# A recurrence beside a mixture of experts on one core: token scaling, loads of B and K, and VectorE's order around Qc are moved

## The chip, the cores and the metric

The kernel runs on one core of one Trainium2 chip. The metric is the device time of one execution in microseconds (us). All inputs start in HBM and the result ends there.

A core has five engines that matter here, each with its own queue of instructions that it works through in order: TensorE (PE; its weight loads are shown as PEld), VectorE (DVE), ScalarE (ACT), GpSimd (POOL) and SyncE (SP), which here only issues DMAs. They wait for each other by semaphores.

## The reference

A delta-rule recurrence (RWKV-7) over 768 tokens runs for 4 batches and 8 heads of dimension 40. Its output, regrouped to 3072 rows of 320, goes through four small two-layer networks whose results are weighted and added.

```python
for t in range(S):                                   # S = 768; B, H, D = 4, 8, 40
    y[:, :, t] = np.einsum('bhd,bhde->bhe', rt, state)
    Sa = np.einsum('bhde,bhe->bhd', state, at)
    state = state * wt[:, :, None, :] - np.einsum('bhd,bhe->bhde', Sa, bt) + np.einsum('bhd,bhe->bhde', vt, kt)
x = y.transpose(0, 2, 1, 3).reshape(B * S, H * D)
p = domain_probs / (domain_probs.sum(-1, keepdims=True) + 1e-09)
for e in range(E):                                   # E = 4, w1[e] 320x1024, w2[e] 1024x320
    out += p[:, e:e + 1] * (np.maximum(x @ w1[e], 0.0) @ w2[e])
```

## The kernel before

**Units.** The recurrence is cut into 12 chunks of 64 tokens. A unit is one chunk of two batches, so there are 24 units (0 to 23), two for each chunk. Inside a unit the recurrence is turned into matrix products. Per unit there are three generators whose pieces are interleaved by hand: `within` (decays, scores, everything that needs no state), `merge` (the inverse of a triangular matrix) and `step` (what needs the state of the unit before).

**Decays.** The raw w of a unit is turned to channels by VectorE (`G`, L520, from the tile `rawW`), multiplied up along the tokens by a scan (L567), and inverted (`1/gp`, L582, 128x512, the reciprocal). From unit 8 on (`BY_CHANNEL`) the raw b and k are turned the same way (`Br`, `Kr`, L638, from `rawB`, `rawK` into the tiles NT and KT) and multiplied by the reciprocal: `N` (L640) and `K` (L644). a is turned and multiplied by the decays (`AT`, L624, and `AG`, L626). Each of rawW, rawB, rawK, rawA is a single tile that is loaded by four DMAs (`load_raw`, L285).

From unit 8 on, b and k are also loaded by tokens (`n_tok`, `k_tok`, L278). They need the same factor: TensorE transposes the reciprocal (pg), ScalarE copies it out (`decay`, L650), and GpSimd multiplies both by it (L727 to L730). That pair of products stands in `substitute`, behind the copies `below` and ahead of the copy of `unit_cols`.

**The triangular inverse.** TensorE makes the scores pfe from AT and NT, ScalarE copies them to F (L669). Two copies on VectorE and two on ScalarE take the diagonal blocks of F (`blocks`, L721). VectorE spreads them (`M`, L733, a transpose to 128x1024) and combines pairs of rows (`Z1`, `Z2`, L745, L749). Then GpSimd substitutes: 48 products and sums on Z (L763, L780). VectorE transposes the result twice (`Qc`, `QTc`, L791, L792) and GpSimd copies it to QT (L798). TensorE uses QTc in pY, Qc in pQ and QT in psat.

**The mixture.** The products of the four networks run on TensorE in pieces between the steps of the recurrence, in "gaps": `gap(n)` of the loop turn u runs one or two pieces. They are made with seven products for two 2x2 block matrices, for which VectorE makes five sums of the hidden values (`a`, L1102) per half expert and adds the results to the output (`osb`, L991). Each piece of w1 is 640 KB (one DMA of 512 KB, two of 64 KB) and is loaded into one of two tiles, w1a and w1b, by DMAs on SP that wait until TensorE has read the piece before.

**What sets the order.** On TensorE the order is that of the program (L110 keeps it). On VectorE a scheduler orders the instructions by its own estimates, but within pairs of the lists at L1433 to L1442: (one, then) means that `then` stands behind `one`. GpSimd's instructions in question are kept in program order. Loads that are put into the list `later` are issued on SP by `begin_later`: a few behind every piece of the mixture (L1184), and the rest where the loop says so. In loop turn u, unit u goes through `step`, unit u+1 through `merge`, unit u+2 through the later pieces of `within` and through `substitute`, and unit u+3 begins. Raw B and K of unit u+3 and W of unit u+4 are put into `later` at the end of turn u, behind `gap(3)`, so they are issued in `gap(0)` of the turn after.

Of the kernel before, what the change touches and what calls it, by code (L numbers as in the profile page):

```python
# [9 lines left out]
ALU = mybir.AluOpType  # L10
# [23 lines left out]
def kernel(  # L34
# [38 lines left out]
    nc = tc.nc  # L73

    B, H, S, D = r.shape
# [5 lines left out]
    NJ = H // 2  # L81
    NF = F // P
    NU = NC * B // 2
# [6 lines left out]
    def noted(ins, name, n=None, i=None):  # L90
        if n is None:
            n = sum(k.startswith(name) for k in made)
        key = f"{name}{n}" if i is None else f"{name}{n}.{i}"
        made[key] = ins
        if key in names:
            stated_order.append(ins)
        return ins
# [24 lines left out]
    def of_mixture(name):  # L122
# [6 lines left out]
        out=ident[:], in_=ident[:], pattern=[[1, P]], compare_op=ALU.is_equal, fill=0.0,  # L129
# [5 lines left out]
    for t, n, op in ((upf, L, ALU.is_gt), (diagf, Q, ALU.is_equal)):  # L135
        nc.vector.memset(t, 1.0)
        for q in range(P // n):
            o = slice(q * n, (q + 1) * n)
            nc.gpsimd.affine_select(
                out=t[o], in_=t[o], pattern=[[1, n]], compare_op=op, fill=0.0, base=0, channel_multiplier=-1,  # L140
# [87 lines left out]
    def pad_raw():  # L228
        for x in "BK":
            nc.gpsimd.memset(room[x][:, :, PAD:2 * D], 0.0)  # L230
# [25 lines left out]
    def begin(u):  # L256
        q = Unit()
        q.u, q.c, q.bp = u, u // (B // 2), u % (B // 2)
        q.b = [2 * q.bp, 2 * q.bp + 1]
        q.start, q.end = q.c == 0, q.c == NC - 1  # L260
        q.apart = u >= EARLY + 2
        q.n = {}
        units.append(q)
        return q
# [57 lines left out]
    def turn_raw(out, t):  # L322

        return nc.vector.transpose(
            out=out.rearrange("p n (x two) -> p n two x", two=2),
            in_=t.rearrange("p n (two e) -> p n two e", two=2)[:, :, :, 0:Q],
        )
# [173 lines left out]
    def within(q):  # L501
# [3 lines left out]
        def pin(ins, also=False):  # L505
            if q.u <= PADDED or also:
                keep(ins)
# [9 lines left out]
            q.G = Gv = flat[:, 0:2 * NJ * L].rearrange("p (c t) -> p c t", t=L)  # L517
            ahead = flat[:, 1:2 * NJ * L + 1].rearrange("p (j i t) -> p i j t", i=2, t=L)
        for i in range(2):
            pin(noted(turn_raw(ahead[:, i], n["rawW"][:, NJ * i:NJ * i + NJ, :]), "G", q.u, i), q.u > EARLY + 2)  # L520
        if by_channel:
            q.gl = G[:, :, L:L + 1]
        else:
# [109 lines left out]
        if by_channel:  # L633
            NT = sb.tile([P, 2 * NJ, L], FP32, name="NT", tag="turned", bufs=3)
            KT = sb.tile([P, 2 * NJ, L], FP32, name="KT", tag="turned", bufs=3)
            for t, x in ((NT, "B"), (KT, "K")):
                for i in range(2):
                    noted(turn_raw(t[:, i::2], n["raw" + x][:, NJ * i:NJ * i + NJ]), x + "r", q.u, i)  # L638
                if x == "B":
                    nc.vector.scalar_tensor_tensor(  # L640
                        out=t[:], in0=t[:], scalar=-1.0, in1=gp[:], op0=ALU.mult, op1=ALU.mult,
                    )
                else:
                    noted(nc.vector.tensor_tensor(out=t[:], in0=t[:], in1=gp[:], op=ALU.mult), "K", q.u)  # L644
        yield
# [70 lines left out]
    def substitute(q, eng, between=None, during=None, first=None):  # L716

        blocks = sb.tile([P, H, Q], FP32, name="blocks")
        for i in range(P // Q):
            move = nc.scalar.copy if i >= 2 else nc.vector.tensor_copy  # L720
            ins = move(out=blocks[quarter(i)], in_=q.F[quarter(i), :, quarter(i % 2)])  # L721
            keep(noted(ins, "blocks", q.u, i))
        run(first)
        q.below = belows()
        for i in (1, 3):
            tc.keep_in_program_order(nc.gpsimd.tensor_copy(out=q.below[quarter(i)], in_=q.F[quarter(i), :, 0:Q]))  # L726
        if q.u >= BY_CHANNEL:  # L727
            for x in (q.N, q.K):
                ins = nc.gpsimd.tensor_tensor(out=x[:, :, 0:D], in0=x[:, :, 0:D], in1=q.decay[:], op=ALU.mult)
                tc.keep_in_program_order(ins)  # L730
        M = sb.tile([P, Q, Q], FP32, name="M")
        cols = blocks[:].rearrange("p h c -> p c h")[:, :, None, :].to_broadcast([P, Q, 4, H])
        ins = nc.vector.transpose(out=M[:], in_=cols)  # L733
        keep(noted(ins, "M", q.u))


        pairs = M[:].rearrange("p (c two) r -> p c two r", two=2)
        on_diag = M[:].rearrange("p c r -> p (c r)")[:, Q + 1::2 * (Q + 1)]
        keep(noted(nc.vector.memset(on_diag, 0.0), "M0", q.u))

        Z = sb.tile([P, 4, Q // 4, Q], FP32, name="Z")
        q.Z = Z[:, 0]
        by_second = Z[:, 1:3].rearrange("p x k r -> p (x k) r")
        below = M[:].rearrange("p c r -> p (c r)")[:, 1::2 * (Q + 1)]
        ins = nc.vector.tensor_tensor(  # L745
            out=by_second, in0=pairs[:, :, 1, :], in1=below[:, :, None].to_broadcast([P, Q // 2, Q]), op=ALU.mult,
        )
        keep(noted(ins, "Z1", q.u))
        ins = nc.vector.tensor_tensor(out=pairs[:, :, 0, :], in0=pairs[:, :, 0, :], in1=by_second, op=ALU.add)  # L749
        keep(noted(ins, "Z2", q.u))  # L750
        run(between)
        at_once = eng is nc.vector
        for x in (0, 3) if at_once else (0,):
            if q.u < 2:
                noted(nc.scalar.copy(out=Z[:, x], in_=unit_cols[:]), "Zu", q.u, x)
            else:
                tc.keep_in_program_order(eng.tensor_copy(out=Z[:, x], in_=unit_cols[:]))
        for j in range(0, Q, 2):
            if during:
                during(j)  # L760
            n, m = j // 4 + 1, Q - 1 - j
            here = 3 * (j // 2 % 2) if at_once else 0
            ins = eng.tensor_tensor(  # L763
                out=Z[:, 1:3, 0:n, j + 1:Q], in0=M[:, j:j + 2, None, j + 1:Q].to_broadcast([P, 2, n, m]),
                in1=Z[:, here, 0:n, j:j + 2].rearrange("p k x -> p x k")[:, :, :, None].to_broadcast([P, 2, n, m]),
                op=ALU.mult,
            )
            noted(ins, "Zm", q.u, j)
            if j == 0:
                tc.keep_in_program_order(ins)  # L770
            z = Z[:, :, 0:n, j + 1:Q]
            if at_once:
                terms = z[:, 0:3] if here == 0 else z[:, 1:4]
                ins = eng.tensor_reduce(
                    out=z[:, 3 - here], in_=terms.rearrange("p x k r -> p k r x"), op=ALU.add, axis=AX.X,
                )
                noted(ins, "Zr", q.u, j)
            else:
                for x in range(1, 3):
                    eng.tensor_tensor(out=z[:, 0], in0=z[:, 0], in1=z[:, x], op=ALU.add)  # L780
        if at_once:

            odd, even = (Z[:, x].rearrange("p k (r four) -> p k r four", four=4)[:, :, :, 1:3] for x in (3, 0))
            eng.tensor_copy(out=even, in_=odd)

    def merge(q):

# [383 lines left out]
    def begin_later(n):  # L1171
        for move in later[:n]:
            tc.keep_in_program_order(move(nc.sync))
        del later[:n]
# [16 lines left out]
    def run(gen, n=99):  # L1191
        if gen is None:
            return
        for _ in range(n):
            if next(gen, gen) is gen:
                break
# [112 lines left out]
    for u in range(1, NU):  # L1309
# [9 lines left out]
        def gap(n, pieces=None):  # L1319
            here[0] = at = 4 * u + n  # L1320
            run(sum_ops, sums_at.get(at, 0))
            mix((1 if at in sparse else 2) if pieces is None else pieces)
# [46 lines left out]
        if u + 3 < NU:  # L1369
# [5 lines left out]
            if u > 1:  # L1375
                later.extend(load_raw(units[u + 3], "VR"))
        run(w, 2)

        soon = u in (2, 3, 4)
        if soon:  # L1380
# [28 lines left out]
        if early:  # L1409
            ws.append(within(units[u + 3]))  # L1410
            run(ws[u + 3], 1)
            if u > 1:
                run(m, 1)
                run(s_next, 1)
            run(m)
            if u == 3:
                begin_later(len(later))
            gap(3, 1)
            run(s_next, 1)
        else:  # L1420
            begin_later(len(later))
            gap(3)
        if BY_CHANNEL <= u + 3 < NU:
            if u + 3 == BY_CHANNEL:
                pad_raw()
            if u >= EARLY + 2 and u + 4 < NU:
                later.extend(load_raw(begin(u + 4), "W"))
            later.extend(load_raw(units[u + 3], "BK"))
        s = s_next
    mix(len(todo))  # L1430
    for piece in last:
# [2 lines left out]
    turned_ahead = [("Qc6", "RT7"), ("RT7", "QTc6")]  # L1434
    turned_ahead += [("QTc6", x) for x in ("VC7.0", "VC7.1", "sum_w15", "sum_w16")]
    waits_of_scalar = [(f"SXc0.{n}", "RTc1.0") for n in range(4)]
    ahead_of_merge = [(f"QTc{u - 1}", f"{x}r{u}.{i}") for u in range(BY_CHANNEL, NU) for x in "BK" for i in range(2)]
    ahead_of_merge += [(f"QTc{u - 1}", f"RH{u - 1}.{r}") for u in range(BY_CHANNEL, NU) for r in range(2)]
    ahead_of_merge += [(f"QTc{u - 1}", f"VC{u}.{r}") for u in range(BY_CHANNEL, NU) for r in range(2)]
    ahead_of_merge += [(f"1/gp{u + 2}", f"sum_a{10 * u - 45 + n}") for u in range(BY_CHANNEL, NU - 2) for n in range(5)]  # L1440
# [34 lines left out]
```

## Time and profile before

| | us |
|---|---|
| median of 3 runs | 1094.14 (1093.46 to 1099.57) |
| the profiled execution | 1094.94 |
| its span, from the first to the last instruction | 1092.8 |
| TensorE busy in the span | 1057.6 (97%) |
| VectorE busy | 812.2 (74%) |
| GpSimd busy | 543.6 (50%) |
| ScalarE busy | 343.3 (31%) |
| mean granted TensorE clock | 0.995 |

The profile is that of one execution. Times in it are us from the start of the span. A line of the timeline gives start, length, engine, line of the kernel, operation, what it writes and reads, shape, and how many instructions of the kind are merged; in brackets stands how long the engine was idle before, and what ended that. The list of waits gives the total of such idle times, how often, and the longest one.

TensorE is busy nearly throughout, so the time is made of its work plus the idle between. The other engines matter where they set that idle, or the order of the work.

### The profile page before, as it was taken

The page shows a single profiled execution, that of the slowest core. Times are in us where ns is not written, and L with a number is a line of the kernel's source. Part 1 is how long each engine was busy: PE and PEld are TensorE (multiplying, and loading weights), DVE is VectorE, ACT ScalarE, POOL GpSimd, SP SyncE. Part 2 cuts the span into 40 slices and gives each one's busy share as a digit, 9 for nine tenths or more (in the row PEclk, how much of TensorE's full clock was granted, in tenths as well). Part 3 has the DMA queues.
Part 4 walks back from the last instruction along what each step waited for, and adds up shares of the span by engine and source line. Part 5 has one row for each costly group of instructions (what it writes and reads, how often), then busy time and mean ns, then how long its engine had stood idle before and what let it go on. Part 6 is the DMA issues. An engine that isn't in the chain of part 4 may idle for free.

```text
span 1092.8 us, 38476 instructions
## 1 busy us (share of the span) xinstructions
PE 1057.6 (97%) x16022; PEld 947.0 (87%) x16022; DVE 812.2 (74%) x1565; ACT 343.3 (31%) x942; POOL 543.6 (50%) x1322
## 2 busy tenths in 40 slices
PE   7999999999999999999999999999999999999998
PEld 7778878989889889999989898898888888988888
DVE  7787779996877978878869788687797877543343
ACT  3433444332323333333323233233232332321110
POOL 6117778756356365465474473744735647430000
PEclk9999999999999999999999999999999999999999
DMA  6876543435443443543553543354444353121220
GB/s 117 213 191 130 136 106 105 106 81 107 118 91 97 106 108 90 112 107 87 119 110 66 131 111 74 84 128 84 101 116 94 87 112 91 38 82 57 67 91 13
DMA packets 275349, 111.04 MB, mean 102 GB/s; under 512 B 229816, under 2 KB 254952, under 8 KB 275176
## 3 DMA queue, kind: packets, MB, share of 16 engines
q1 hardware_dynamic: 271192, 107.75, 42.5%
q8 instruction: 126, 2.06, 0.8%
q10 hardware_dynamic: 3984, 0.84, 0.4%
q14 instruction: 47, 0.39, 0.1%
HBM read 100.65 MB, written 3.93 MB: 96 GB/s over the span
## 4 chain that ended last, share of the span: by engine, by line
PE 49%; POOL 27%; DVE 14%; issue 6%; SPq 2%; DMA 1%; ACT 1%; DVEq 0%; POOLq 0%; ACTq 0%
PE ph L110 21%; PE p L110 17%; POOL Z L780 17%; POOL Z L763 10%; DVE a L1102 3%; DVE M L733 3%; PE prn L110 2%; PE po L110 2%; DVE blocks L721 1%; DVE osb L991 1%; PE pdy L110 1%; DVE M L749 1%; DVE Z L745 1%; PE pY L110 1%; DVE Qc L791 1%
## 5 line engine op out<-in xcount | busy, mean ns | idle before, releaser
L780 POOL TENSOR_TENSOR Z<-Z 128x31 f32<-128x31 f32 (+7 forms) x704 | 257.9, 366 | 55.1
L110 PE MATMUL ph<-xT,w1b 128*128 128x256 f32 (+3 forms) x1536 | 225.1, 377 | 0.5 <-issue 0.5
L110 PE MATMUL ph<-xT,w1a 128*128 128x256 f32 (+3 forms) x1536 | 222.7, 375 | 0.0
L1102 DVE TENSOR_TENSOR a<-hs 128x512 f32<-128x512 f32 x220 | 159.6, 749 | 78.2 <-ACT hs L976 78.2
L976 ACT ACTIVATE hs<-ph 128x512 f32<-128x512 f32 (+1 forms) x208 | 116.5, 564 | 311.2 <-PE ph L110 309.2
L763 POOL TENSOR_TENSOR Z<-M,Z 128x62 f32<-128x62 f32 (+7 forms) x352 | 148.6, 422 | 100.1 <-DVE M L749 74.3
L110 PEld LDWEIGHTS ph<-xT,w1b 128*128 128x128 f32 (+1 forms) x1536 | 170.3, 163 | 28.8 <-issue 7.0
L110 PEld LDWEIGHTS ph<-xT,w1a 128*128 128x128 f32 (+1 forms) x1536 | 169.0, 162 | 29.0 <-issue 7.3
L110 PE MATMUL p<-sums,a 128*128 128x160 f32 x1056 | 164.9, 299 | 0.0
L991 DVE SCALAR_TENSOR_TENSOR osb<-p,gate,osb 128x320 f32<-128x320 f32 (+1 forms) x243 | 107.2, 479 | 64.3 <-PE p L110 61.0
L110 PEld LDWEIGHTS p<-sums,a 128*128 128x128 f32 x1056 | 152.8, 190 | 2.2
L726 POOL COPY below<-F 32x256 f32<-32x256 f32 x48 | 30.5, 636 | 202.5 <-ACT F L669 167.9
L110 PEld LDWEIGHTS p<-w,hs 128*128 128x128 f32 x704 | 98.6, 190 | 8.5 <-issue 7.3
L110 PE MATMUL p<-w,hs 128*128 128x160 f32 x704 | 104.9, 302 | 0.0
L110 PE MATMUL p<-w,a 128*128 128x160 f32 x704 | 102.8, 299 | 0.0
L110 PEld LDWEIGHTS p<-w,a 128*128 128x128 f32 x704 | 98.0, 190 | 0.0
L798 POOL COPY QT<-QTc 32x256 f32<-32x256 f32 x96 | 44.0, 458 | 60.6 <-DVE QTc L792 54.3
L896 ACT COPY RS<-pxr 64x256 f32<-64x256 f32 x88 | 32.3, 367 | 112.2 <-DVE SX L499 77.5
L791 DVE STREAM_TRANSPOSE Qc<-Z 128x256 f32<-128x256 f32 x24 | 14.9, 621 | 54.4 <-POOL Z L780 54.3
L582 DVE RECIPROCAL gp<-G 128x512 f32<-128x512 f32 x16 | 53.6, 3352 | 0.5
L707 ACT COPY EV<-pev 64x160 f32<-64x160 f32 x96 | 23.1, 286 | 83.0 <-PE pev L110 82.6
L733 DVE STREAM_TRANSPOSE M<-blocks 128x1024 f32<-128x1024 f32 x24 | 47.4, 1976 | 2.3 <-ACT blocks L721 0.6
(167 smaller groups left out, 1440.2 us busy)
## 6 DMA issues: line engine op xcount, KB each, us to landing
w1a<-in_moe_w_dram SPq DMA_DIRECT2D x37, 512.0 KB
w1b<-in_moe_w_dram SPq DMA_DIRECT2D x37, 512.0 KB
w<-in_moe_w_dram SPq DMA_DIRECT2D x4, 1280.0 KB
w1a<-in_moe_w_dram SPq DMA_DIRECT2D x74, 64.0 KB
w1b<-in_moe_w_dram SPq DMA_DIRECT2D x74, 64.0 KB
out_dram<-osb SPq DMA_DIRECT2D x45, 80.0 KB
rawW<-in_w_dram SPq DMA_DIRECT2D x48, 72.0 KB
natV<-in_v_dram SPq DMA_DIRECT2D x42, 80.0 KB
```

Of the source, the lines that this page charges most:

```text
L110: return stated(nc.tensor.matmul(**k))
L582: pin(noted(nc.vector.reciprocal(out=gp[:], in_=G[:, :, 1:L + 1]), "1/gp", q.u))
L726: tc.keep_in_program_order(nc.gpsimd.tensor_copy(out=q.below[quarter(i)], in_=q.F[quarter(i), :, 0:Q]))
L733: ins = nc.vector.transpose(out=M[:], in_=cols)
L763: ins = eng.tensor_tensor(out=Z[:, 1:3, 0:n, j + 1:Q], in0=M[:, j:j + 2, None, j + 1:Q].to_broadcast([P, 2, n, m]), in1=Z[:, here, 0:n, j: ...
L780: eng.tensor_tensor(out=z[:, 0], in0=z[:, 0], in1=z[:, x], op=ALU.add)
L791: keep(noted(nc.vector.transpose(out=dealt(Qc[:]), in_=q.Z), "Qc", q.u))
L798: ins = nc.gpsimd.tensor_copy(out=q.QT[quarter(i), :, quarter(i % 2)], in_=QTc[quarter(i)])
L896: nc.scalar.copy(out=RS[half(s), x ^ s::2], in_=prs[x][half(s)].rearrange("p (j i) t -> p j i t", i=2),)
L976: ins = nc.scalar.activation(out=h[:, i * HF // 2:(i + 1) * HF // 2, 0:n], in_=ph[i][:], func=ACTF.Relu,)
L991: ins = nc.vector.scalar_tensor_tensor(out=to, in0=p, scalar=sc, in1=to, op0=ALU.mult, op1=ALU.add)
L1102: ins = nc.vector.tensor_tensor(out=t[:], in0=x, in1=y, op=op)
```

## The change

GpSimd's products of n_tok and k_tok leave `substitute` and become the function `scale_tokens`. It is called in loop turn u for unit u+2, behind the copies of QT of unit u+1. The products so stand ahead of `below` of unit u+2 instead of behind it.

Raw B and K of unit u+3 are put into `later` ahead of `gap(3)` of turn u instead of behind it. W of unit u+4 is still put there behind `gap(3)`.

On VectorE the pairs of the stated order change, from unit 8 on:

- N and K of unit u now stand ahead of Qc of unit u-1. Before, the turns of b and k had to stand behind QTc of unit u-1.
- G of unit u stands ahead of Qc of unit u-2 (from unit 11 on). Before, it was kept in program order.
- The reciprocal of unit u+1 stands behind VC of unit u and behind RH of unit u-1.

```diff
-            pin(noted(turn_raw(ahead[:, i], n["rawW"][:, NJ * i:NJ * i + NJ, :]), "G", q.u, i), q.u > EARLY + 2)
+            pin(noted(turn_raw(ahead[:, i], n["rawW"][:, NJ * i:NJ * i + NJ, :]), "G", q.u, i), EARLY + 2 < q.u < BY_CHANNEL + 3)
...
                 if x == "B":
-                    nc.vector.scalar_tensor_tensor(
+                    ins = nc.vector.scalar_tensor_tensor(
                         out=t[:], in0=t[:], scalar=-1.0, in1=gp[:], op0=ALU.mult, op1=ALU.mult,
                     )
+                    noted(ins, "N", q.u)
...
-        if q.u >= BY_CHANNEL:
-            for x in (q.N, q.K):
-                ins = nc.gpsimd.tensor_tensor(out=x[:, :, 0:D], in0=x[:, :, 0:D], in1=q.decay[:], op=ALU.mult)
-                tc.keep_in_program_order(ins)
...
+    def scale_tokens(q):
+        for x in (q.N, q.K):
+            ins = nc.gpsimd.tensor_tensor(out=x[:, :, 0:D], in0=x[:, :, 0:D], in1=q.decay[:], op=ALU.mult)
+            tc.keep_in_program_order(ins)
...
         run(w, 2)
+        if BY_CHANNEL <= u + 2 < NU:
+            scale_tokens(units[u + 2])
...
             begin_later(len(later))
+            if BY_CHANNEL <= u + 3 < NU:
+                if u + 3 == BY_CHANNEL:
+                    pad_raw()
+                later.extend(load_raw(units[u + 3], "BK"))
             gap(3)
-        if BY_CHANNEL <= u + 3 < NU:
-            if u + 3 == BY_CHANNEL:
-                pad_raw()
-            if u >= EARLY + 2 and u + 4 < NU:
-                later.extend(load_raw(begin(u + 4), "W"))
-            later.extend(load_raw(units[u + 3], "BK"))
+        if u >= EARLY + 2 and u + 4 < NU:
+            later.extend(load_raw(begin(u + 4), "W"))
...
-    ahead_of_merge = [(f"QTc{u - 1}", f"{x}r{u}.{i}") for u in range(BY_CHANNEL, NU) for x in "BK" for i in range(2)]
+    ahead_of_merge = [(f"{x}{u}", f"Qc{u - 1}") for u in range(BY_CHANNEL, NU) for x in "KN"]
+    ahead_of_merge += [(f"G{u}.{i}", f"Qc{u - 2}") for u in range(BY_CHANNEL + 3, NU) for i in range(2)]
+    ahead_of_merge += [(f"VC{u}.{r}", f"1/gp{u + 1}") for u in range(BY_CHANNEL, NU - 1) for r in range(2)]
+    ahead_of_merge += [(f"RH{u - 1}.{r}", f"1/gp{u + 1}") for u in range(BY_CHANNEL, NU - 1) for r in range(2)]
     ahead_of_merge += [(f"QTc{u - 1}", f"RH{u - 1}.{r}") for u in range(BY_CHANNEL, NU) for r in range(2)]
```

## The prediction

> **What bounds the kernel now.** Read first: TensorE's busy time in windows cut at the first pY matmul of each unit. The window from the pY of unit k to the pY of unit k+1 is called stretch k here, and +x means x us after its start. Three of them, starting at units 12, 16 and 17 (columns: window, length, then busy time of PE, PEld, DVE, ACT, POOL; granted clock; DMA):
>
> ```profile
> core 0: us, PE busy (x) PEld busy (x) DVE busy (x) ACT busy (x) POOL busy (x), PEclk, DMA share, GB/s
> 486.55:528.10 41.55, 41.55 (x674) 37.94 (x666) 33.42 (x64) 13.75 (x39) 23.57 (x58) 1.00 0.40 89
> ...
> 660.67:705.06 44.39, 42.30 (x660) 38.18 (x661) 35.08 (x65) 13.76 (x38) 24.28 (x58) 1.00 0.40 87
> 705.06:749.75 44.69, 43.17 (x660) 39.40 (x661) 34.96 (x65) 13.87 (x38) 24.33 (x58) 0.97 0.49 111
> ```
>
> Stretch 12 is TensorE from end to end: 41.55. Stretch 16 has 2.1 of idle; stretch 17 follows that idle, gets a lower clock, and needs 1.6 more for the same matmuls. Stretches 8 to 21 together last 610.04 and hold 591.46 of TensorE work, so at most some 19 to 22 (with 41.7 to 42.3 per stretch) can be had here. What TensorE waits for, in the list of its waits:
>
> ```profile
> PE pY L110 <- DVE QTc L792: 19.8, 14, 2.1
> ```
>
> All of it is one wait. Third, the timeline of one stretch (16), the chain that ends in that wait:
>
> ```profile
> 667.42 3.35 DVE L582 RECIPROCAL gp<-G 128x512 f32<-128x512 f32 x1
> ...
> 671.65 0.55 DVE L991 SCALAR_TENSOR_TENSOR osb<-p,gate,osb 128x320 f32<-128x320 f32 x1 [0.50 <-PE p L110]
> ...
> 672.29 0.65 ACT L669 COPY F<-pfe 128x256 f32<-128x256 f32 x2 [4.39 <-PE pfe L110]
> ...
> 672.70 4.83 DVE L1102 TENSOR_TENSOR a<-hs 128x512 f32<-128x512 f32 x5
> 677.45 0.77 DVE L721 COPY blocks<-F 32x256 f32<-32x256 f32 x2
> 678.32 1.97 DVE L733 STREAM_TRANSPOSE M<-blocks 128x1024 f32<-128x1024 f32 x1
> ...
> 682.05 0.29 POOL L763 TENSOR_TENSOR Z<-M,Z 128x62 f32<-128x62 f32 x1 [4.26 <-DVE M L749]
> ...
> 703.82 0.61 DVE L791 STREAM_TRANSPOSE Qc<-Z 128x256 f32<-128x256 f32 x1 [3.74 <-POOL Z L780]
> ...
> 705.06 0.37 PE L110 MATMUL pY<-QTc,below 64*64 64x64 f32 x2 [2.10 <-DVE QTc L792]
> ```
>
> F is there at 672.94 (+12.3), but blocks starts at 677.45: N, G, K and the reciprocal held VectorE until 670.77, so the five sums a run late and stand in front of blocks. From M on nothing is loose: GpSimd waits for M (4.26), Qc for Z, TensorE for QTc. GpSimd has scaled n_tok and k_tok (674.53 to 676.98) before those 4.26 of idle: the scaling is not on the chain.
>
> **The change, part by part.** TensorE's and ScalarE's orders are unchanged; VectorE, GpSimd and SP change from the stretches around unit 8 on.
>
> 1. *N, K, G go ahead of Qc.* After QTc, VectorE loses NT 0.73, N 0.65, G 0.76, scan 1.23, KT 0.74, K 0.69: 4.8. The reciprocal then runs from +2.2 (RH ends there) to +5.6 instead of to +10.1; the sums a start when ScalarE delivers hs (+7.2) and are done, with their osb, before the last osb, which waits for TensorE's p at +11.0. In the new order the last three are osb, a, osb: 0.47 + 0.60 + 0.30, to +12.4; F is ready at +12.3; blocks take 0.7. So M starts at +13.2. Stretch 22 shows this place already: it has no G and no reciprocal, and M starts at 939.82, 13.1 after its 926.68. Before, M was at +14.3 (11), +16.4 (13), +17.7 (16), +18.1 (15). Gain: 1 to 5.
>
> 2. *What steps in.* With VectorE free early, the new order puts AT's transpose and product between M and the steps Z1 and Z2 that GpSimd waits for. Stretch 10 has this order already:
>
> ```profile
> 417.42 1.97 DVE L733 STREAM_TRANSPOSE M<-blocks 128x1024 f32<-128x1024 f32 x1
> 419.31 0.67 DVE L324 STREAM_TRANSPOSE AT<-rawA 128x512 f32<-128x512 f32 x1
> ...
> 420.02 0.69 DVE L626 TENSOR_TENSOR AT<-AT,G 128x512 f32<-128x512 f32 x1
> ...
> 422.18 0.29 POOL L763 TENSOR_TENSOR Z<-M,Z 128x62 f32<-128x62 f32 x1 [3.81 <-DVE M L749]
> ```
>
> M to GpSimd's start: 4.76, against 3.73 in stretch 16: 1.0 given back. In stretches 10, 14, 18 VT's transpose (0.65) stands there as well. Substitution starts at +18.0, in those three at +18.6 (before: +18.0 to +21.8).
>
> 3. *Contention.* N, K and in even stretches G's scan now run beside GpSimd's substitution. No row shows them there; nearest rows:
>
> ```profile
> 615.72 2.17 POOL L798 COPY QT<-QTc 32x256 f32<-32x256 f32 x4 [1.26 <-DVE QTc L792]
> 616.94 0.69 DVE L640 SCALAR_TENSOR_TENSOR NT<-NT,gp 128x512 f32<-128x512 f32 x1
> ...
> 660.65 1.73 POOL L798 COPY QT<-QTc 32x256 f32<-32x256 f32 x4 [1.26 <-DVE QTc L792]
> ...
> 204.46 1.47 POOL L780 TENSOR_TENSOR Z<-Z 128x54 f32<-128x54 f32 x2
> 204.53 1.31 DVE L566 TENSOR_TENSOR_SCAN G<-G,first 128x512 f32<-128x512 f32 x1
> ...
> 640.38 0.68 POOL L780 TENSOR_TENSOR Z<-Z 128x54 f32<-128x54 f32 x2
> ```
>
> N beside the QT copies costs GpSimd 2.17 - 1.73 = 0.44; the scan 1.47 - 0.68 = 0.8; a product of K's kind 0.4 (AT's product at 682.56: the Z pair at 682.42 takes 0.94, the unhindered 29-wide pair at 683.80 0.57). Taken: N and K 0.84, with scan 1.64. Bounds: 0, and the full durations 0.69 + 0.69 + 1.24 = 2.62. Substitution alone is 21.5 (stretch 10, AT's product outside it). So it ends at +18.0 + 21.5 + 0.84 = +40.35 in odd stretches, +41.15 in even ones, +41.75 in 10, 14, 18.
>
> The Trainium skill, "SBUF — State Buffer", section "Who interferes with whom", speaks against this part: it says a VectorE instruction with two SBUF inputs contends with a GpSimd instruction that reads SBUF, and that whichever starts first keeps the other out entirely. By that the price would be the 2.62; the rows show some six tenths of the durations.
>
> 4. *Behind the substitution.* From the last Z to pY is 1.26 (703.80 to 705.06). In stretches 9, 11, ... 19 the new order has G's scan between Qc and QTc: +1.15 (1.24, less 0.09 of overlap). In 9, 13, 17 Qc is also queued behind osb, KT, K and G's transposes, which wait for TensorE's p (+37.2, as at 565.33 in stretch 13): 1.01 + 0.70 + 0.30 + 0.62 + 0.30 + 0.65 put Qc at +40.8, 0.4 later than Z allows. In even stretches KT, K, G and scan fit into the idle that VectorE has before those osb and before Qc (1.48 and 3.74 in stretch 16).
>
> 5. *GpSimd's scaling behind the QT copies.* It runs at +1.8 to +3.6, where GpSimd waited 10.6 for F: nothing on the path. Its inputs n_tok and k_tok were issued until +42.1 (702.81) and, now earlier on SP, land well before. Cover gone would cost nothing before +12.3. It clears blocks (1.81 beside n_tok in stretch 15, 0.77 in 16), which is in the 13.2.
>
> 6. *Raw B and K a gap sooner, W behind them.* Six transfers fill SP's idle time between two weight loads (680.09 to 687.61, +19.4 to +26.9), two and W's four follow the second load (+28.7 to +31.5). xT, A, V and R move up by about 3. Landings: a four-part load issued until 405.24 releases its reader at 406.96, 1.7 later. The B turns come at +22.5 at the earliest, the K turns at +32.5 (10, 14, 18) or from +35.6, the G turns from +37. Cost 0; a late landing is the slow rival below.
>
> Sum per stretch (last Z + 1.26, + 1.15 with scan): 9, 13, 17: 43.15; 11, 15, 19: 42.75; 21 (no G): TensorE's 41.7; 8, 12, 16, 20: 42.4; 10, 14, 18: 43.0. Together 129.45 + 128.25 + 41.7 + 169.6 + 129.0 = 598.0 against 610.04: -12.0. Stretch 6 (43.12 long, 42.34 of TensorE work) gets N and K beside its substitution (+0.85), stretch 7 loses its wait (-0.8). TensorE still waits 1.0 to 1.5 in odd stretches, 0.1 to 0.8 in even ones. The profiled execution took 1094.94 (span 1092.8): 1082.9; the median of the runs, 1094.14, is 0.8 lower: 1082.
>
> The clock: three of the four idles of 2.08 to 2.12 are followed by about 3.4 us at half clock, which costs 1.6 each; the one of 2.08 and all of 1.5 are not. The forecast has none above 1.5, so the three (5 us) go, and this is within the 598.0. The Trainium skill, "TensorE: Matmul & The Clock Gate", section "Why this matters for your kernels", allows idle gaps up to about 3 us; these rows show the drop at 2.1, so the row is taken. By the rule there would be no drop in either kernel.
>
> **Rivals.** *TensorE becomes the bound* (12%): contention near its lower bound and no scan on the path in effect; 14 stretches at 41.7 or 42.3 (seven each) are 588: 1072. For it: stretches 11 and 12 run so. Against it: the scan between Qc and QTc is in the order.
> *Given back* (17%): full lock, +1.0 in seven even stretches and about +0.5 in odd ones, +9: 1091; with two clock drops in 9, 13, 17 (their 1.5 is near 2.1) 1094: a stall that only moves. For it: the skill's rule. Against: the rows of 3.
> *Late landings* (7%, slower): VectorE works in order, so a K or G turn whose transfer hasn't landed holds Y, the state and Qc. K's last two pieces follow a load of 640 KB. A landing at +41.5, 12 after the issue, would put Qc behind K and G at about +43.5: +2.5 on 13 stretches, 1114. It decides from about 7 us between issue and landing (4.5 in 10, 14, 18). For it: SP and the queues are shared with the weights. Against: 1.7 above.
> Slower by several lesser things: 4%.
>
> **How the numbers follow.** The forecast, 1082, has 60%; its own range, from half the contention to the full price on even stretches alone, is 1077 to 1088. About what a measurement here can tell from no change is 0.5%, 5.5 us: faster is below 1088.7, slower above 1099.6. Faster: 60 + 12 + 4 of the 17 = 76%. Same: 13%. Slower: 11%. The range takes in the bound of TensorE (1072) and the given-back case (1091) with a little over: 1072 to 1092.
>
> **What would show it.** M at +13 in stretches 9 to 21; substitution starting at +18.0 to +18.6 and 22.3 to 23.2 long; waits of pY for QTc of 1.0 to 1.5 (odd) and under 0.8 (even), with no clock drop; GpSimd's scaling at +2 to +4; no wait of VectorE on a raw transfer. Wrong if substitution exceeds 24 or starts behind +19.5, or if Qc waits for VectorE's own queue by over 1 us in even stretches.

## The result, and the profile after

The changed kernel takes 1079.29 us (median of 4 runs, 1078.46 to 1080.12) against 1094.34 for the kernel before on the same chip: a ratio of 0.9853, with a 95% interval of 0.982 to 0.9885. The forecast was 1082. The profiled execution took 1080.12, its span is 1078.4 (before: 1092.8). Stretches 8 to 21 together last 594.88 instead of 610.04: 15.2 less, where the forecast had 12.0. The span fell by 0.7 less than these stretches: 0.46 were lost ahead of them and 0.27 behind.

Windows of stretches 12, 16 and 17 of the kernel after (columns as in the windows shown of before):

```profile
core 0: us, PE busy (x) PEld busy (x) DVE busy (x) ACT busy (x) POOL busy (x), PEclk, DMA share, GB/s
...
486.93:528.87 41.94, 41.80 (x660) 38.20 (x661) 33.01 (x65) 13.86 (x38) 23.47 (x57) 1.00 0.42 91
...
656.92:700.15 43.23, 41.78 (x660) 38.18 (x661) 32.90 (x65) 13.86 (x38) 24.52 (x58) 1.00 0.42 88
700.15:743.09 42.94, 41.82 (x660) 38.09 (x661) 32.90 (x65) 13.86 (x38) 22.86 (x58) 1.00 0.51 116
```

Stretch 12, which was the good one before, is 0.4 longer; 16 and 17 are 1.2 and 1.8 shorter. The clock is 1.00 in all of them, and TensorE's own work is 41.8 in stretches of both kinds. The list of TensorE's waits has the same wait at its head, now 11.0 instead of 19.8, and nowhere above 1.5:

```profile
PE pY L110 <- DVE QTc L794: 11.0, 12, 1.5
```

The chain in stretch 14 (pY at 571.71), from the timeline; this answers to the stretches 16 and 10 shown of before:

```profile
583.75 0.38 DVE L993 SCALAR_TENSOR_TENSOR osb<-p,minus_gate,osb 128x160 f32<-128x160 f32 x1
584.06 0.69 DVE L722 COPY blocks<-F 32x256 f32<-32x256 f32 x2
...
584.90 1.97 DVE L730 STREAM_TRANSPOSE M<-blocks 128x1024 f32<-128x1024 f32 x1 [0.16 <-ACT blocks L722]
...
587.50 0.69 DVE L626 TENSOR_TENSOR AT<-AT,G 128x512 f32<-128x512 f32 x1
...
588.71 0.71 DVE L324 STREAM_TRANSPOSE VT<-rawV 128x512 f32<-128x512 f32 x1
...
590.14 0.29 POOL L760 TENSOR_TENSOR Z<-M,Z 128x62 f32<-128x62 f32 x1 [4.63 <-DVE M L746]
```

All sums stand ahead of the last osb, blocks follows it at once, and M starts at +13.2. AT's product and VT's turn then stand between M and GpSimd's first Z, at +18.4. At the end of stretch 12 the scan, K and N run beside the substitution; in front of the pY of stretch 16 (656.92), at the end of the odd stretch 15, the scan stands between Qc and QTc. Two more pieces of the timeline:

```profile
523.29 0.72 DVE L645 TENSOR_TENSOR KT<-KT,gp 128x512 f32<-128x512 f32 x1
523.53 0.65 POOL L760 TENSOR_TENSOR Z<-M,Z 128x70 f32<-128x70 f32 x1
...
524.72 1.26 DVE L566 TENSOR_TENSOR_SCAN G<-G,first 128x520 f32<-128x520 f32 x1
524.96 1.08 POOL L760 TENSOR_TENSOR Z<-M,Z 128x48 f32<-128x48 f32 x1
```

```profile
654.78 0.63 DVE L793 STREAM_TRANSPOSE Qc<-Z 128x256 f32<-128x256 f32 x1
655.26 1.18 DVE L566 TENSOR_TENSOR_SCAN G<-G,first 128x520 f32<-128x520 f32 x1
656.35 0.42 DVE L794 STREAM_TRANSPOSE QTc<-Qc 128x256 f32<-128x256 f32 x1
```

The same two steps of Z, 70 and 48 wide, take 0.33 and 0.27 where nothing hinders them (stretch 16): K costs GpSimd 0.32, the scan 0.81. The scan puts QTc 0.91 behind where it would start.

Lengths of the stretches against the forecast:

| stretches | before | forecast | after |
|---|---|---|---|
| 9, 13, 17 | 43.2 to 44.7 | 43.15 | 42.83, 42.84, 42.94 |
| 11, 15, 19 | 41.6 to 44.9 | 42.75 | 42.28, 42.30, 42.27 |
| 8, 12, 16, 20 | 41.6 to 44.4 | 42.4 | 42.00, 41.94, 43.23, 41.95 |
| 10, 14, 18 | 42.4 to 44.4 | 43.0 | 42.73, 42.91, 43.09 |
| 21 | 44.9 | 41.7 | 41.58 |

So the time fell as the steps said, nearly stretch by stretch. Whether it fell for the reason that they gave is another question, and the experiments answer: only in part.

### The profile page after: what moved, and what is told of

Same layout as the page of the kernel before. It is cut to its first block, busy times and chain, and to the rows that moved or that the text cites. A ratio compares the mean times of both kernels' runs of the same rounds, so it can differ in the third digit from the quotient of the medians.

```text
span 1078.4 us, 38527 instructions
## 1 busy us (share of the span) xinstructions
PE 1052.9 (98%) x16022; PEld 945.3 (88%) x16022; DVE 793.6 (74%) x1565; ACT 344.4 (32%) x942; POOL 536.6 (50%) x1322
## 4 chain that ended last, share of the span: by engine, by line
PE 65%; POOL 14%; DVE 8%; issue 5%; DMA 4%; SPq 2%; ACT 2%; DVEq 0%; ACTq 0%; POOLq 0%
PE ph L110 27%; PE p L110 19%; POOL Z L777 8%; POOL Z L760 5%; PE po L110 3%; PE pdy L110 2%; PE prn L110 2%; PE psat L110 1%; PE pxr L110 1%; PE pfe L110 1%; PE pY L110 1%; PE pQ L110 1%; PE warm L110 1%; SPq L404 1%; DVE osb L993 1%
## 5 line engine op out<-in xcount | busy, mean ns | idle before, releaser
L777 POOL TENSOR_TENSOR Z<-Z 128x31 f32<-128x31 f32 (+7 forms) x704 | 261.3, 371 | 55.1
L1104 DVE TENSOR_TENSOR a<-hs 128x512 f32<-128x512 f32 x220 | 152.3, 710 | 102.6 <-ACT hs L978 102.6
L110 PE MATMUL ph<-xT,w1b 128*128 128x256 f32 (+3 forms) x1536 | 222.6, 374 | 0.5 <-issue 0.5
L760 POOL TENSOR_TENSOR Z<-M,Z 128x62 f32<-128x62 f32 (+7 forms) x352 | 158.6, 450 | 112.0 <-DVE M L746 86.2
L727 POOL COPY below<-F 32x256 f32<-32x256 f32 x48 | 20.7, 432 | 174.0 <-ACT F L670 172.3
L800 POOL COPY QT<-QTc 32x256 f32<-32x256 f32 x96 | 40.4, 421 | 68.5 <-DVE QTc L794 60.6
L670 ACT COPY F<-pfe 128x256 f32<-128x256 f32 x48 | 15.5, 376 | 80.1 <-PE pfe L110 79.0
```

Source lines behind the costliest of these rows:

```text
L110: return stated(nc.tensor.matmul(**k))
L760: ins = eng.tensor_tensor(out=Z[:, 1:3, 0:n, j + 1:Q], in0=M[:, j:j + 2, None, j + 1:Q].to_broadcast([P, 2, n, m]), in1=Z[:, here, 0:n, j: ...
L800: ins = nc.gpsimd.tensor_copy(out=q.QT[quarter(i), :, quarter(i % 2)], in_=QTc[quarter(i)])
L1104: ins = nc.vector.tensor_tensor(out=t[:], in0=x, in1=y, op=op)
```

## The experiments

Twelve kernels in three groups, each group beside its own runs of the kernel before (1095.26, 1095.26 and 1094.45); after stands against the 1094.34 above. "8 to 21" is the length of those fourteen stretches in the profiled execution, "M" the start of M's transpose in stretches 16 and 17 (before: +17.65 and +17.85).

| kernel | median us | ratio to before, interval | 8 to 21 | M, 16 and 17 |
|---|---|---|---|---|
| after | 1079.29 | 0.985 (0.982 to 0.989) | 594.9 | 13.5, 13.2 |
| e1 scaling alone | 1081.18 | 0.987 (0.986 to 0.989) | 596.4 | 16.3, 15.4 |
| e2 loads alone | 1084.24 | 0.990 (0.989 to 0.992) | 598.9 | 14.3, 15.5 |
| e3 order alone | 1085.69 | 0.992 (0.990 to 0.994) | 601.2 | 13.1, 13.1 |
| e4 order and loads | 1078.93 | 0.985 (0.984 to 0.987) | 594.6 | 13.5, 13.1 |
| e5 after, G not ahead | 1067.93 | 0.975 (0.974 to 0.977) | 582.6 | 13.2, 13.2 |
| e6 after, N and K not ahead | 1071.38 | 0.979 (0.977 to 0.980) | 586.3 | 13.2, 13.2 |
| e7 after, reciprocal free | 1106.53 | 1.011 (1.009 to 1.013) | 621.1 | 13.2, 14.6 |
| e8 after, scan behind QTc | 1068.85 | 0.976 (0.975 to 0.978) | 584.3 | 13.2, 13.2 |
| e9 after, AT behind Z2 | 1075.23 | 0.983 (0.981 to 0.984) | 590.2 | 13.5, 13.2 |
| e11 scaling and loads | 1079.54 | 0.987 (0.985 to 0.989) | 594.2 | 14.3, 14.8 |
| e14 as e5, and AT behind Z2 | 1066.02 | 0.974 (0.972 to 0.976) | 581.7 | 13.2, 13.2 |
| e16 before, no scaling | 1080.42 | 0.988 (0.986 to 0.989) | 594.7 | 16.3, 15.4 |

### The scaling alone (e1), and left out (e16)

On the kernel before, only the function is moved:

```diff
-        if q.u >= BY_CHANNEL:
-            for x in (q.N, q.K):
-                ins = nc.gpsimd.tensor_tensor(out=x[:, :, 0:D], in0=x[:, :, 0:D], in1=q.decay[:], op=ALU.mult)
-                tc.keep_in_program_order(ins)
...
         run(w, 2)
+        if BY_CHANNEL <= u + 2 < NU:
+            scale_tokens(units[u + 2])
```

> The kernel before with one part of the change: GpSimd's scaling of n_tok and k_tok moves behind the copies of QT; loads and VectorE's order stay. Theory A (the scaling was in VectorE's way in before: beside it the two copies of blocks took 1.81 instead of 0.69 in stretches 9, 13, 15, 17, 19, 21, and the five sums a took 4.83 instead of about 3.3 in 14, 16, 18, 20): M comes 1.1 to 1.4 earlier in these ten stretches, TensorE's waits of 2.1 shrink to about 0.9, the clock drops go; 1094.3 falls to about 1083 (1079 to 1087). Theory B (as the prediction had it, the scaling is not on the chain by itself): 1094 (1092 to 1096), M where it was.

For e16 the four lines are only taken out. That kernel leaves the factor of b and k by tokens out altogether, so it only bounds what the scaling costs.

> The kernel before with GpSimd's two products of n_tok and k_tok left out (so b and k by tokens go without the factor; nothing else changes). It bounds what the scaling costs where before has it. Theory A (all of its price is what it does to blocks and the sums; moved behind the copies of QT it costs nothing more): 1081, as with the move alone, within 1.5. Theory B (at its new place it still slows VectorE's N, K and scan, 0.4 to 0.7 in a stretch): 1074 to 1078. Theory C (the gain of the move came from something else, such as GpSimd's order): 1090 or more.

Theory A in both: 1081.18 and 1080.42. The one move that the prediction put off the chain gives 14.1 of the 15 by itself, with VectorE's order in stretches 14 to 21 exactly as before, and taking the products out altogether gives no more than moving them (the difference of 0.8 is inside the spread of the runs). How it acted is seen in before's own timeline, first stretch 16, then 15:

```profile
672.70 4.83 DVE L1102 TENSOR_TENSOR a<-hs 128x512 f32<-128x512 f32 x5
...
674.53 1.19 POOL L729 TENSOR_TENSOR n_tok<-n_tok,decay 128x320 f32<-128x320 f32 x1
675.67 1.31 POOL L729 TENSOR_TENSOR k_tok<-k_tok,decay 128x320 f32<-128x320 f32 x1
...
677.45 0.77 DVE L721 COPY blocks<-F 32x256 f32<-32x256 f32 x2
```

```profile
631.50 1.18 POOL L729 TENSOR_TENSOR n_tok<-n_tok,decay 128x320 f32<-128x320 f32 x1
631.88 1.81 DVE L721 COPY blocks<-F 32x256 f32<-32x256 f32 x2
632.64 0.90 POOL L729 TENSOR_TENSOR k_tok<-k_tok,decay 128x320 f32<-128x320 f32 x1
```

and the same place in e1, stretch 16 (pY at 655.76):

```profile
667.80 3.69 DVE L1103 TENSOR_TENSOR a<-hs 128x512 f32<-128x512 f32 x5
...
671.41 0.57 DVE L721 COPY blocks<-F 32x256 f32<-32x256 f32 x2
672.09 1.98 DVE L729 STREAM_TRANSPOSE M<-blocks 128x1024 f32<-128x1024 f32 x1
```

The five sums take 3.69 without the scaling beside them instead of 4.83, and in the odd stretch the two copies of blocks take 0.8 instead of 1.81. M so comes 1.3 earlier in stretch 16, and the stretch falls by the same 1.3, from 44.39 to 43.05. TensorE's longest wait for QTc falls from 2.1 to 0.8, so the clock no longer drops behind it: TensorE's own work falls by 1.4 to 1.6, the larger part of what stretches 15, 17 and 21 gain (44.7 to 44.9 before, 42.4 in e1).

The Trainium skill, "SBUF — State Buffer", section "Who interferes with whom", says that a VectorE instruction with two inputs in SBUF meets GpSimd's reads, and that a copy can enter a mode that takes the port they share. Both the sums, which have two such inputs, and the copies are slower in these rows; whether the copies were in that mode no run shows. The prediction held that rule against the new overlap of its third step; of the same overlap in the kernel before it names blocks (fifth step), but not the sums, and it gave the scaling no price there.

### The loads alone (e2), and with the scaling (e11)

```diff
             begin_later(len(later))
+            if BY_CHANNEL <= u + 3 < NU:
+                if u + 3 == BY_CHANNEL:
+                    pad_raw()
+                later.extend(load_raw(units[u + 3], "BK"))
             gap(3)
-        if BY_CHANNEL <= u + 3 < NU:
-            if u + 3 == BY_CHANNEL:
-                pad_raw()
-            if u >= EARLY + 2 and u + 4 < NU:
-                later.extend(load_raw(begin(u + 4), "W"))
-            later.extend(load_raw(units[u + 3], "BK"))
+        if u >= EARLY + 2 and u + 4 < NU:
+            later.extend(load_raw(begin(u + 4), "W"))
```

> The kernel before with the loads alone: raw B and K begun a gap sooner and W behind them. With the data earlier the scheduler itself puts K right behind N and the reciprocal ahead of every sum; N, K, G and the scan still stand behind QTc. Theory A (place on VectorE decides): the reciprocal ends at about +9.5, M at about +15.5, the substitution starts at +20.3 with 21.5 of its own, stretches of 43.0: about 1088 (1085 to 1092). Theory B (loads are hidden, so they do nothing): 1094.

> The kernel before with the scaling moved and the loads sooner, and none of the new pairs on VectorE. Theory A (against the loads alone, only the odd stretches gain, where blocks took 1.5 beside the scaling; the even ones keep 42.5, TensorE's work and 0.65 that pQ waits for VC behind N and K): odd stretches 42.2 to 42.6, 1077.5 (1074 to 1080). Theory B (the pairs on VectorE are needed): 1082 to 1085, as with the loads alone.

The loads are not free of effect, though no row waits less for a transfer: 1084.24, a little under the range of theory A. The scheduler orders VectorE by its own estimate of when data comes, so earlier loads alone put K right behind N, and the sums between the osb, where before has four osb and then all five sums in a row in front of blocks (even stretches from 14 on). The reciprocal has ended by +9.5. Even stretches fall to 42.5, of which 0.65 is a new wait, of TensorE's pQ for VC, which has slipped behind N and K. Odd stretches stay at 43.0 to 43.4, because blocks still takes 1.5 beside the scaling. With the scaling moved too, the odd ones are at 42.4 to 42.7: 1079.54, theory A, and about as fast as the whole change with none of its pairs.

### VectorE's order without the loads (e3), and with them but with the scaling where it was (e4)

e3 is the kernel after with the old loop for the loads and the old place of the scaling, e4 with the old place of the scaling alone.

> The kernel after without its loads and without its scaling: VectorE's new pairs alone. N and K of the next unit then stand right in front of Qc, behind the last osb, and their raw data is issued from +31 to +39. Theory A (the earlier loads are what makes the order possible): K's turn waits for its transfer until about +41, Qc comes at +42 or later, TensorE waits 1.5 to 2.5 in nearly every stretch: about 1093 (1088 to 1100), with clock drops. Theory B (the order alone carries the gain): 1079 to 1083.

> The kernel after with the scaling put back behind the copies below; VectorE's order and loads stay. Theory A (in the new order the scaling falls beside M's transpose at +13.4 to +15.2 and beside nothing that it slows): 1079.3, within 1.5. Theory B (the scaling slows blocks or AT's product here too, by 0.5 to 1.1 in a stretch): 1083 to 1090.

e4 is theory A: 1078.93, the same as after. In the new order the sums and blocks are done at +13.0, and the scaling (+13.4 to +15.1) meets nothing but M's transpose, which takes 1.99 beside it and 1.97 without. So the order with the loads, and the move, each take away that overlap. Either is enough, and the other then adds little: nothing to e4, some 2 to e1. The order does more than that, and spends it again. GpSimd's first Z in stretch 16 of e1:

```profile
675.82 0.29 POOL L759 TENSOR_TENSOR Z<-M,Z 128x62 f32<-128x62 f32 x1 [5.48 <-DVE M L745]
```

It is at +20.1 there and at +18.25 in after, but from it to the last Z there are 21.7 in e1 and 23.7 in after: the 1.8 that the order wins ahead of the substitution is lost in it.

e3 is between its theories, and theory A was wrong in its reason. 1085.69, not 1093. The end of stretch 14 (pY of 15 at 617.78):

```profile
614.53 0.69 DVE L640 SCALAR_TENSOR_TENSOR NT<-NT,gp 128x512 f32<-128x512 f32 x1
615.14 0.77 DVE L324 STREAM_TRANSPOSE KT<-rawK 128x256 f32<-128x256 f32 x2
615.94 0.69 DVE L645 TENSOR_TENSOR KT<-KT,gp 128x512 f32<-128x512 f32 x1
616.55 0.61 DVE L792 STREAM_TRANSPOSE Qc<-Z 128x256 f32<-128x256 f32 x1
```

No brackets: neither b's nor k's turn waits for its transfer. GpSimd's last Z ended at 615.3, and Qc stands 1.3 behind it only because N and K are in front of it in VectorE's queue. All stretches from 8 to 20 are 43.0 to 43.1 long. In e4, with the loads sooner, N and K stand further ahead, and at the end of the same stretch Qc waits for Z again:

```profile
612.61 0.61 DVE L792 STREAM_TRANSPOSE Qc<-Z 128x256 f32<-128x256 f32 x1 [0.83 <-POOL Z L781]
```

So what the sooner loads change here is the place that the scheduler gives to N and K. How far ahead N and K could have stood with the old loads, whose last piece is issued at 612.4, no run shows.

### Which of the three pairs is needed (e5, e6, e7)

e5 takes the pair of G out of the kernel after, e6 puts the old pair in for N and K, e7 takes out the two of the reciprocal:

```diff
-    ahead_of_merge += [(f"G{u}.{i}", f"Qc{u - 2}") for u in range(BY_CHANNEL + 3, NU) for i in range(2)]
```

```diff
-    ahead_of_merge = [(f"{x}{u}", f"Qc{u - 1}") for u in range(BY_CHANNEL, NU) for x in "KN"]
+    ahead_of_merge = [(f"QTc{u - 1}", f"{x}r{u}.{i}") for u in range(BY_CHANNEL, NU) for x in "BK" for i in range(2)]
```

```diff
-    ahead_of_merge += [(f"VC{u}.{r}", f"1/gp{u + 1}") for u in range(BY_CHANNEL, NU - 1) for r in range(2)]
-    ahead_of_merge += [(f"RH{u - 1}.{r}", f"1/gp{u + 1}") for u in range(BY_CHANNEL, NU - 1) for r in range(2)]
```

(In e5 G is also held in program order again, as in the kernel before.)

> The kernel after without the pair that puts G ahead of Qc: G's turns and the scan stand behind RH again, ahead of the reciprocal. Theory A (G and scan cost the chain more where they are now, 0.55 beside the substitution in even stretches and 0.9 between Qc and QTc in odd ones, than the 2.0 that they take off the reciprocal, which then runs from +4.2 to +7.6 and still leaves M at about +13.5): every stretch falls to TensorE's 41.8 or a little over, 1069 to 1073. Theory B (G has to be out of the way for M to come at +13): M at +15, stretches of 43 to 43.5, 1082 to 1088.

> The kernel after with b's and k's turns held behind QTc as before, all else as after. Theory A (the move of N and K ahead of Qc is not needed, since the reciprocal then ends at about +7.2, just as hs comes, and the substitution is rid of 0.7 of contention): stretches of 41.8 to 42.2, 1070 to 1075. Theory B (N and K ahead of Qc are the gain, as the prediction had it): M at +15 or later, 1085 or more.

> The kernel after without the pairs that hold the reciprocal behind VC and RH. In odd units it then stands between Qc and QTc, in even ones between QTc and VC. Theory A (those pairs guard QTc and VC): QTc comes 2.2 to 3.3 later at the end of odd stretches, with a clock drop behind it, and pQ waits about 1.8 for VC in the others: 1095 to 1115. Theory B (the place of the reciprocal is free within these bounds): 1078 to 1083.

Theory A in all three, with e5 1.1 under its range. Without G ahead the kernel is about 11 faster than after, without N and K ahead about 8; each of the two moves that the prediction's first step counted as the gain is, beside the other, a loss. (No run takes back both and keeps the pairs of the reciprocal; e11, which has none of the pairs, is at 1079.54.) e5, stretch 17 (pY at 692.25):

```profile
694.44 0.76 DVE L324 STREAM_TRANSPOSE G<-rawW 128x256 f32<-128x256 f32 x2
695.24 1.59 DVE L566 TENSOR_TENSOR_SCAN G<-G,first 128x520 f32<-128x520 f32 x1
696.86 3.35 DVE L582 RECIPROCAL gp<-G 128x512 f32<-128x512 f32 x1
...
705.45 1.98 DVE L730 STREAM_TRANSPOSE M<-blocks 128x1024 f32<-128x1024 f32 x1 [0.16 <-ACT blocks L722]
```

The reciprocal ends 2.4 later than in after, at +8.0, and M starts at the same +13.2: the sums wait for ScalarE's hs until +7.2, and blocks can't start before F, at +12.3. In after VectorE is idle between the reciprocal and the first sum, here in stretch 15:

```profile
621.88 1.29 DVE L1104 TENSOR_TENSOR a<-hs 128x512 f32<-128x512 f32 x2 [1.73 <-ACT hs L978]
```

e5 fills that idle with G and the scan, which in after cost GpSimd 0.81 or QTc 0.91. With N and K behind QTc (e6) the reciprocal ends at +7.0 to +8.2, the substitution in odd stretches takes 21.4 instead of 22.1, and these fall to 41.6. In 10, 14 and 18 the reciprocal ends latest, M starts at +13.5, and the scan is still beside the substitution: 42.4.

The pairs of the reciprocal guard against something that the other pairs make possible. In e7 with G done early it is ready before Qc, and stands between Qc and QTc at the end of the even stretches (the expectation had the odd ones); the end of 16 (pY of 17 at 716.77), and then the window of stretch 15, which follows such a wait:

```profile
712.42 0.63 DVE L793 STREAM_TRANSPOSE Qc<-Z 128x256 f32<-128x256 f32 x1
712.96 3.35 DVE L582 RECIPROCAL gp<-G 128x512 f32<-128x512 f32 x1
716.23 0.39 DVE L794 STREAM_TRANSPOSE QTc<-Qc 128x256 f32<-128x256 f32 x1
...
716.77 0.97 PE L110 MATMUL pY<-QTc,below 64*64 64x64 f32 x13 [3.22 <-DVE QTc L794]
```

```profile
627.57:671.78 44.21, 43.37 (x661) 39.63 (x661) 29.79 (x64) 13.87 (x38) 23.28 (x58) 0.96 0.48 111
```

TensorE waits 3.2 to 3.4 seven times, and each time the next stretch's work takes 1.4 to 1.6 more, at a lower clock: 1106.53.

### What TensorE still waits for (e8, e9, e14)

e8 adds to the kernel after that the scan stands behind QTc, e9 has AT and VT behind Z2 in place of M, e14 is e9's line in e5:

```diff
+    ahead_of_merge += [(f"QTc{u - 2}", f"scan{u}") for u in range(BY_CHANNEL + 3, NU)]
```

```diff
-    ahead_of_merge += [(f"M{u}", f"AT{u + 1}") for u in range(BY_CHANNEL, NU - 1)]
+    ahead_of_merge += [(f"Z2{u}", f"{x}{u + 1}") for u in range(BY_CHANNEL, NU - 1) for x in ("AT", "VT")]
```

> The kernel after with one more pair: the scan of G stands behind QTc of the substitution it now runs beside or behind. It falls into the 1.2 of idle that VectorE has before RH. Theory A (the scan is most of what TensorE still waits for: 0.55 beside the substitution in even stretches, 0.9 between Qc and QTc in odd ones): all stretches at 41.8 to 42.0, 1069 to 1072. Theory B (the rest of the wait comes from AT between M and Z2, 1.0): odd stretches fall by 0.5 to 0.9 only, even ones with VT stay near 42.5, 1074 to 1077.

> The kernel after with AT's and VT's turns held behind Z2 instead of behind M. Theory A (this is the 1.0, with VT 1.5, that the prediction gave back in its second step; AT's product then runs beside the substitution and costs 0.5 of it): substitution from +17.0, even stretches at TensorE's 41.6 to 41.9, odd ones 41.8 to 42.4: 1071 (1069.5 to 1073.5). Theory B (VectorE's queue in front of Qc sets the end of the odd stretches 9, 13, 17 whatever the substitution does, and contention eats the rest): 1075 or more.

> The kernel after without the pair of G and with AT and VT behind Z2: both of the changes that should help, together. Theory A (without G ahead, TensorE already works nearly without a wait, 41.53 in most stretches, so what comes off the substitution's start is hidden): 1067.5 (1066 to 1069). Theory B (there is still a wait to be had): below 1066.

e8 is theory A, 1068.85, 0.2 under its range. The scan lies in the idle that VectorE has before RH, and both prices of it are gone: 41.6 in even stretches, 41.9 in odd ones. e9 is theory B, at its edge: the substitution starts 1.0 earlier and the even stretches fall to 41.8 to 42.3, but it is 0.8 longer there, since AT's product now runs beside its first steps, and the odd ones don't move (42.83 in 9 and 13, as in after), because Qc stands behind osb and K until +40.7 and the scan behind that. AT between M and Z2 was only a price where nothing else was later.

e14 is the fastest: 1066.02, at the lower edge of theory A, not told apart from e5 by the intervals of the two. Its windows of stretches 15 and 16, and TensorE's wait:

```profile
608.00:649.53 41.53, 41.53 (x673) 37.79 (x666) 34.05 (x64) 13.86 (x39) 23.26 (x58) 1.00 0.50 121
649.53:691.07 41.54, 41.54 (x674) 37.93 (x666) 34.04 (x64) 13.85 (x39) 23.32 (x57) 1.00 0.42 91
```

```profile
PE pY L110 <- DVE QTc L794: 1.2, 1, 1.2
```

In stretches 8 to 21 TensorE shows no gap any more; the one wait left is in front of stretch 7. So this profile shows no idle there that a better order of VectorE or GpSimd could take away: the 14 stretches last 581.7, and TensorE is busy in all of it.

## Why the prediction was right, and where it was not

*First step, the order frees VectorE and M comes at +13.2.* The place was right: M starts at +13.19 to +13.20 in every stretch from 9 to 21 but 16 (+13.49: VectorE is idle there for 0.46 before M instead of 0.16, though ScalarE's half of blocks ends no later; why is open). The reason holds in part: e4, with the order and the loads and the scaling where it was, has the whole gain. But "N, G, K and the reciprocal held VectorE until 670.77, so the five sums a run late and stand in front of blocks" left out why they took 4.83. e1 keeps that order, brings M 1.3 earlier in stretch 16 and gets 14.1. And e5 and e6 show that G did not have to leave where N and K did, nor N and K where G did.

*Second step, AT and VT between M and Z2.* Right: the substitution starts at +17.96 to +18.01 and, with VT, at +18.43 (forecast +18.0, +18.6); in 16 at +18.25.

*Third step, contention.* Right in kind, mis-sized: K 0.32 where 0.4 was taken, N some 0.4 for 0.44, the scan 0.81 for 0.8, but on a substitution of 21.4 by itself the whole comes to 0.7 to 0.85 (forecast 0.84) in odd and to 1.3 in even stretches (1.64), 22.7 instead of 23.15; in 10, 14 and 18 it takes 23.0 to 23.2. Stretch 16 has 23.7, and 23.6 in e4 as well: the substitution begins 0.3 later there, and the same instructions of VectorE meet other steps of Z. The 2.62 of a full exclusion is not seen.

*Fourth step, behind the substitution.* The scan costs 0.91 where 1.15 was taken, since it overlaps Qc by more. Qc is queued until +40.7 in 9, 13, 17 as said. With the third step this is the 3.1 by which the fourteen stretches beat the forecast.

*Fifth step, "nothing on the path".* This is the step that failed. In the order of after it is true (e4), but in the order of before the scaling lengthened the five sums by 1.1 in the even stretches from 14 on and blocks by 1.0 in most odd ones, and that was worth 14.1 by itself (e1). The prediction had the row (blocks 1.81 beside n_tok, 0.77 otherwise) and booked it as part of the first step's 13.2, and it took the 4.83 as the sums' own time: without the scaling beside them they take 3.69.

*Sixth step, loads.* No price, as said, but "no wait of VectorE on a raw transfer" was too much: in 10, 14 and 18 the turns of b wait 0.5 to 0.6 and those of k 1.2 to 2.0 for data. In 10 and 14 Qc waits for Z behind them, so it costs nothing. In 18 the queue has no idle left behind the turn of k, and Qc starts 0.47 behind the last Z, which ended at 784.49:

```profile
777.33 0.77 DVE L324 STREAM_TRANSPOSE KT<-rawK 128x256 f32<-128x256 f32 x2 [1.95 <-DMA rawW<-in_w_dram]
...
784.96 0.59 DVE L793 STREAM_TRANSPOSE Qc<-Z 128x256 f32<-128x256 f32 x1
```

So there the late transfer costs some 0.4. That the loads alone would change VectorE's order (e2) was not foreseen.

*Stretches 6 and 7* went by +0.9 and -0.9 (forecast +0.85 and -0.8), and no clock drop is left in the stretches from 8 on.

*The rivals.* TensorE is not the bound of the kernel after: of its 594.9 in these stretches 10.1 are still waiting. The floor of that rival was also mis-sized, 588 for what is 581.7 in e14: the 42.3 of TensorE's work in even stretches goes with the order of before (e1 has it too), and is about 41.8 in after and 41.5 to 41.6 in e14; why is not shown. So the waits behind 10, 14, 16 and 18 are 0.96 to 1.45, where under 0.8 was forecast for even stretches; in odd ones they are 0.5 to 1.1 for 1.0 to 1.5. The stall was not given back, and of late landings only that of stretch 18 shows a price.

So the forecast was close because its place for M was right and the sum was made from there. What it said about the parts of the change was wrong: the scaling alone, or the order with the loads, would have been enough, each with nearly the whole gain, and G, or N and K, ahead of Qc took back 8 to 11 of what could be had (13 with AT and VT moved too, e14). Left open is why e11's profiled execution lost some 3 in the first two units, which no part of the change touches, and why the steps of Z met by a product of VectorE lose only some half of its duration.

## What to carry to other kernels

When an instruction takes longer in one place than elsewhere, find what runs beside it before explaining why it starts late; a neighbour on another engine that "isn't on the chain" can be its cause, and moving that neighbour is cheaper than reordering. When parts of a change can each remove the same stall, run each alone: here they gave 14.1, 11.0 and 9.6, and together 15. And moving work off an engine's early stretch is worth only what the next data's arrival leaves (F at +12.3 here); beyond that it only spends cover somewhere else.

## What the hardware showed beyond that

- Only some of VectorE's instructions hinder GpSimd's substitution. Over the 16 substitutions of stretches 6 to 21 of the kernel after, take the steps of Z that have one kind of VectorE instruction beside them, each against the second shortest duration of the same step: 29.4 us of osb (one input in PSUM) lengthened these by 0.2 in all, 6.0 of RT's turns by 0.06, 6.1 of K's turns by 0.04, but 14.9 of the sums by 5.5 and 1.6 of N by 1.2. The scan's effect shows in the rows above.
- It works the other way as well: a copy of VectorE from SBUF to SBUF, 32x256, takes 0.9 beside GpSimd's product of 128x320 and 0.35 without, while M's transpose of 128x1024 takes 1.99 to 2.02 beside it and 1.97 without.
- The clock: e3's 13 waits of 1.27 to 1.31 are followed by no slower stretch, e7's seven of 3.2 to 3.4 all are. With before's rows (2.08 no, 2.10 and 2.12 yes) the Trainium skill, "TensorE: Matmul & The Clock Gate", section "Why this matters for your kernels", with its gaps up to about 3 us, is too wide for this case.
